# One bank left out before the value tiles, the branch to the exact maxima ahead of its tile's router steps, the last value tile copied by VectorE

## The chip, the core and the metric

The kernel runs on one core of one Trainium2 chip. The metric is the device time of one execution, in microseconds (us); of several executions the median counts. The engines are named as in the profile: PE (TensorE, the matrix unit; PEld are its weight loads), ACT (ScalarE), DVE (VectorE), POOL (GpSimd) and SP (SyncE, which here only issues DMAs). PSUM is the memory that PE writes; it has eight banks, and a tile of 128 partitions by 512 f32 fills one.

## The reference, cut to what is computed

The input x has 2048 tokens of width 1024. Three things come from it:

```
a = softmax(q k^T * 32^-0.5) v  @ wo      32 heads of width 32, q, k, v = x @ wqkv
b = sum over 32 heads of gelu(x . u[e]) * v[e],  e = the best of 64 experts
    (argmax of q1 k1^T over 8, argmax of q2 k2^T over 8)
g = sigmoid(sum(x * gate_w));   out = g * a + (1 - g) * b
```

## The kernel before, in words

All matmuls up to the attention are made in split precision: an operand is a high and a low part, and three products (high by high, high by low, low by high) are summed in one PSUM bank. x stays in SBUF as xh and xl. Tokens are cut into 16 tiles of 128 (NT = 16), the contraction into 8 chunks of 128 (KC = 8). A token tile therefore costs 8 x 3 = 24 matmuls of 128x128 by 512.

The stages follow each other in the order in which they are written; every engine works through its own instructions in that order, and semaphores tie the engines together.

1. q and k (lines 192 to 357): 16 chunks of 128 columns, each for four pieces of 512 tokens.
2. Router (lines 394 to 528): for each token tile t, `router_mm` (L394) makes the scores in a PSUM bank (matmuls at L401), and `router_step` (L450) makes four steps on DVE, ACT and POOL for the tiles t, t-1, t-2 and t-3. The step for tile t itself, `router_1` (L404 to L417), reads the bank: ACT copies a part (L405), DVE takes the maxima (L409 to L414). After tile 4 a bound on the attention scores is computed (`bound`). After tile 8 comes `exact_maxima` (L482): every engine loads that bound into a register (L484) and branches (L486). Only if the bound is above a limit does a loop over the heads run that takes exact maxima. With these inputs it isn't entered.
3. Values (lines 550 to 644): two halves of 512 columns. `values` (L550) makes the 24 matmuls of a tile (L558), `values_out` (L561) copies the bank to SBUF on ACT (L564; two buffers "vo") and issues the store on ACT's queue. In each half the first four tiles are made together, chunk by chunk (L619, L638). In the first half the last four (fin0, L626) are made together too. Between the halves ACT and DVE split the weights of the second half (`split_wv`, L631); only then, in ACT's order, are fin0's four banks copied (L636). The last tile of the second half is made in a bank of another pool (L643 and L644, tile "o"), because the pool ps1 with its eight banks is closed at L642.
4. Attention (lines 664 to 892): scores in a ring of seven banks (L714), exponentials on ACT (L724), the products with the values (L735).
5. Output projection (from L895).

PSUM banks are given out in turn by a counter (L97 to L102):

```
def bank():
    i = bank_no[0] % 8
    bank_no[0] += 1
    return ps1.tile([128, 512], F32, name=f"bk{i}")
```

A tile of a bank's name waits for the readers of that name's last tile. The stages up to the router take 80 banks, the router one for each tile and three beside (two in `bound`, one in `gate_sums`). The body of `exact_maxima` takes 65 (64 in its inner loops and one for a transpose) when the program is written, whether the branch is taken or not. At L637 the counter is rounded up to a multiple of eight. The tile "o" is the only one of a PSUM pool that is opened from the right end; the pools ps1 and the ring are laid from the left.

Of the kernel before, what the change touches and what calls it, by code (L numbers as in the profile page):

```python
# [9 lines left out]
F32 = mybir.dt.float32  # L10
F32R = mybir.dt.float32r
I32 = mybir.dt.int32
AF = mybir.ActivationFunctionType
# [7 lines left out]
NT = S // 128  # L21
# [9 lines left out]
def gated_mha_peer_kernel(ctx, tc, xT, wqkv, wv, wo, wq, k12, ug, v, out):  # L31
# [8 lines left out]
    nc = tc.nc  # L40
# [28 lines left out]
    def dma(dst, src, queue=nc.sync):  # L69
        a, b = (ap.bitcast(F32) if ap.dtype == F32R else ap for ap in (dst, src))  # L70
        return queue.dma_start(a, b)  # L71
# [16 lines left out]
    def split(hi, lo, src, on=None):  # L88
        nc.scalar.activation(hi, src, AF.Copy)  # L89
        (on or nc.vector).tensor_tensor(out=lo, in0=src, in1=hi.bitcast(F32), op=OP.subtract)  # L90
# [5 lines left out]
    ps1 = Pool("ps1", space=PSUM)  # L96
    bank_no = [0]  # L97
# [5 lines that stand above are left out]
# [215 lines left out]
    for k, (w, c) in enumerate(chunks):  # L318
        hi, lo = whl.pop((w, c))
        for n in range(NQ):  # L320
            ps = bank()
# [72 lines left out]
    def router_mm(t):  # L394
        ps = bank()
        for kc in range(KC):
            tok = slice(t * 128, (t + 1) * 128)
            wh, wl = Wp[kc]
            for a, b, first, last in ((xh, wh, kc == 0, False), (xh, wl, False, False),
                                      (xl, wh, False, kc == KC - 1)):  # L400
                nc.tensor.matmul(ps, a[:, kc, tok], b, start=first, stop=last)  # L401
        RT[t] = ps
# [47 lines left out]
    def router_step(t):  # L450
        for lag, f in ((3, router_4), (2, router_3), (1, router_2), (0, router_1)):
            if 0 <= t - lag < NT:
                f(t - lag)

    def bound():
        pb = bank()
        nc.tensor.matmul(pb[:H, 0:1], prf, ones[:, 0:1], start=True, stop=True)
        pb2 = bank()
        nc.tensor.matmul(pb2[:1, :H], ones[:, 0:1], prf, start=True, stop=True)
        nc.vector.tensor_reduce(cbits, pb2[:1, :H], axis=AX.X, op=OP.max)  # L460
        cneg = bw.tile([H, 1], F32, name="cneg")
        nc.scalar.activation(cneg, pb[:H, 0:1], AF.Copy, scale=-1.0)
        for r in range(2):
            sh = bw.tile([H, 512], F32R, name=f"sh{r}", bufs=1)
            if r == 0:
                nc.vector.tensor_copy(sh, cneg.to_broadcast([H, 512]))
            else:
                nc.vector.memset(sh.bitcast(F32), 0.0)
            dma(SHD[:, r, :].rearrange("h (n s) -> h n s", n=4), sh[:, None, :].to_broadcast([H, 4, 512]))

    def gate_sums():
        pz = bank()
        for qc in range(NQ):
            nc.tensor.matmul(pz[32 * qc:32 * qc + 32, :], ones, zacc[:, qc * 512:(qc + 1) * 512],
                             start=True, stop=True)
        zs = bw.tile([128, 512], F32, name="zs", bufs=1)
        nc.scalar.activation(zs, pz, AF.Copy)
        for qc in range(NQ):
            dma(ZD[:, qc * 512:(qc + 1) * 512], zs[32 * qc:32 * qc + 1, :])


    def exact_maxima():  # L482
        limit_bits = int(np.float32(SHIFT_LIMIT / SCALE).view(np.int32))
        creg = nc.values_load(cbits.bitcast(I32), min_val=0, max_val=2 ** 31 - 1,  # L484
                              skip_runtime_bounds_check_because="a float's bits without its sign")
        with tc.If(creg > limit_bits):  # L486
            with ExitStack() as st:
                gp = st.enter_context(tc.tile_pool(name="gp", bufs=1))
                with tc.For_i(0, H, 1) as h:
                    kt = gp.tile([96, S], F32R, name="gk")  # L490
                    hs, rows = bass.ds(h, 1), bass.ds(h * 32, 32)
                    for i, part in enumerate((0, 0, 1)):
                        dma(kt[32 * i:32 * i + 32, :], QKD[1][part][rows, :])
                    mx = gp.tile([128, NT, 4], F32, name="mx")
                    for t in range(NT):
                        if t % 8 == 0:
                            qt = gp.tile([96, S // 2], F32R, name="gq")
                            c = slice(t * 128, (t + 8) * 128)
                            for i, part in enumerate((0, 1, 0)):
                                dma(qt[32 * i:32 * i + 32, :], QKD[0][part][rows, c])  # L500
                        for n in range(4):
                            ps = bank()
                            nc.tensor.matmul(ps, qt[:, t % 8 * 128:(t % 8 + 1) * 128], kt[:, n * 512:(n + 1) * 512],
                                             start=True, stop=True)
                            nc.vector.tensor_reduce(mx[:, t, n:n + 1], ps, axis=AX.X, op=OP.max)
                    mr = gp.tile([128, NT], F32, name="mr")
                    nc.vector.tensor_reduce(mr, mx, axis=AX.X, op=OP.max, negate=True)
                    pt = bank()
                    nc.tensor.transpose(pt[:NT, :128], mr, ident)
                    hi = gp.tile([NT, 128], F32R, name="ghi")  # L510
                    lo = gp.tile([NT, 128], F32R, name="glo")
                    split(hi, lo, pt[:NT, :128])
                    for r, src in ((0, hi), (1, lo)):
                        dma(SHD[hs, r:r + 1, :].rearrange("a b (t s) -> (a b t) s", t=NT), src)

    for t in range(NT - 1):
        router_mm(t)
        router_step(t)
        if t == 4:
            bound()  # L520
        if t == 5:
            gate_sums()
            rz.close()
        if t == 8:
            exact_maxima()
    router_mm(NT - 1)
    rw.close()

# [21 lines left out]
    def values(ts, half, bank=bank):  # L550
        ps = [bank() for _ in ts]
        for kc in range(KC):
            wh, wl = WV[half, kc]
            for t, p in zip(ts, ps):
                tok = slice(t * 128, (t + 1) * 128)
                for a, b, first, last in ((xh, wh, kc == 0, False), (xh, wl, False, False),
                                          (xl, wh, False, kc == KC - 1)):
                    nc.tensor.matmul(p, a[:, kc, tok], b, start=first, stop=last)  # L558
        return ts, ps, half

    def values_out(ts, ps, half):  # L561
        for t, p in zip(ts, ps):
            o = vw.tile([128, 512], F32, name="vo")
            nc.scalar.activation(o, p, AF.Copy)  # L564
            dma(VD[half][t * 128:(t + 1) * 128, :], o, nc.scalar)

    def peer_act():
# [36 lines left out]
    def peer_turn(Ahl):  # L604
        for n in range(NQ):
            pt = bank()
            for t in range(4):
                nc.tensor.transpose(pt[:, t * 128:(t + 1) * 128],  # L608
                                    Ahl[:, 4 * n + t, :].bitcast(F32), ident)
            at = vw.tile([128, 512], F32R, name="at", bufs=1)  # L610
            nc.scalar.activation(at, pt, AF.Copy)
            dma(ATD[:, n * 512:(n + 1) * 512], at)
# [4 lines left out]
    zt = sm2.tile([NT, 128], F32, name="zt")  # L617
    dma(zt, ZD.rearrange("o (b m) -> (o b) m", m=128))
    values_out(*values(list(range(4)), 0))  # L619
    for t in range(4, NT - 4):  # L620
        values_out(*values([t], 0))
        if t == 5:
            Ahl = peer_act()
        if t == 10:
            peer_turn(Ahl)
# [8 lines left out]
    load_kq(0, Z)  # L634
    load_shift(0, Z)
    values_out(*fin0)  # L636
    bank_no[0] += -bank_no[0] % 8  # L637
    values_out(*values(list(range(4)), 1))  # L638
    for t in range(4, NT - 1):
        values_out(*values([t], 1))  # L640

    ps1.close()  # L642
    pso = Pool("pso", space=PSUM, side="right")  # L643
    values_out(*values([NT - 1], 1, lambda: pso.tile([128, 512], F32, name="o")))  # L644
    vw.close()
    sm2.close()
    sm.close()
# [403 lines left out]
```

## Time and profile before

| | |
|---|---|
| median of 3 runs | 1893.1 us (1891.32 to 1894.84) |
| profiled execution: its time, its span | 1894.6 us, 1892.8 us |
| PE busy | 1875.8 us (99%) |
| ACT busy | 1158.7 us (61%) |
| DVE busy | 1202.2 us (64%) |
| mean granted clock of TensorE | 0.998 |
| router's matmuls (L401), first and last start | 391.6 and 484.1 us |
| values' matmuls (L558), first and last start | 484.4 and 667.1 us |

Times in the trace count from the start of the span. A timeline row reads: start, duration, engine, line, operation, output <- input, shape, count, and in brackets how long the engine had been idle and who ended that. A row of a window gives for each engine the busy time in it and the number of instructions, and then PEclk, the clock granted to TensorE (1.00 is full). Matmuls overlap: one is shown with 0.39 us, but the next starts 0.23 us later.

### The profile page before, as it was taken

How to read it: one execution, taken by the hardware profiler on the slowest of the kernel's cores; microseconds unless marked ns; L12 is line 12 of the kernel's file. 1: busy time of each engine (PE TensorE's matmuls, PEld its weight loads, DVE VectorE, ACT ScalarE, POOL GpSimd, SP SyncE). 2: the span in 40 equal slices, each digit the busy share in tenths (PEclk: the TensorE clock that was granted, in tenths of full speed). 3: DMA queues.
4: the chain of work that ended last, by engine and by line, in shares of the span. 5: the costliest groups of instructions: out<-in, count | busy, mean ns of one | idle time of the engine just before them, and what ended most of it. 6: DMA issues, size and time to landing. Idle time of an engine off the chain costs nothing.

```text
span 1892.8 us, 25742 instructions
## 1 busy us (share of the span) xinstructions
PE 1875.8 (99%) x10271; PEld 1157.9 (61%) x10271; DVE 1202.2 (64%) x916; ACT 1158.7 (61%) x1413; POOL 148.6 (8%) x183
## 2 busy tenths in 40 slices
PE   9999999999998999999999999999999999999999
PEld 7877777887887844444444444444444444448887
DVE  4522224866520068888888888888888888895220
ACT  4211111200121189999999999999999999993110
POOL 0000000035200000000000000000000000010000
PEclk9999999999999999999999999999999999999999
DMA  5777774420222167777777776877777777756521
GB/s 211 278 270 254 264 271 137 137 73 2 79 88 79 46 161 166 160 172 159 175 169 183 167 184 157 184 162 184 170 176 170 164 166 179 188 128 172 154 89 67
DMA packets 108082, 302.72 MB, mean 160 GB/s; under 512 B 14724, under 2 KB 48660, under 8 KB 84472
## 3 DMA queue, kind: packets, MB, share of 16 engines
q1 hardware_dynamic: 70520, 154.76, 27.4%
q0 software_dynamic: 14976, 103.29, 26.3%
q10 hardware_dynamic: 22464, 43.00, 7.0%
q8 instruction: 81, 1.33, 0.3%
q14 instruction: 41, 0.34, 0.1%
HBM read 138.73 MB, written 62.66 MB: 106 GB/s over the span
## 4 chain that ended last, share of the span: by engine, by line
PE 76%; ACT 0%; DMA 0%; ACTq 0%; issue 0%; DVE 0%
PE ring L714 28%; PE o L735 25%; PE pa L918 9%; PE bk L558 9%; PE bk L401 2%; PE ring L748 1%; PE pa L927 1%; PE o L558 0%; ACT P L724 0%; PE o L748 0%; ACT vo L564 0%; DMA vd<-vo 0%; PE bk L608 0%; ACT accd L724 0%; ACTq L71 0%
## 5 line engine op out<-in xcount | busy, mean ns | idle before, releaser
L724 ACT ACTIVATE P<-ring 128x512 f32<-128x512 f32 (+2 forms) x1034 | 914.5, 984 | 14.9 <-PE o L735 1.4
L763 DVE TENSOR_TENSOR acc<-acc,P 128x2048 f32<-128x2048 f32 x319 | 730.9, 2291 | 74.1 <-ACT P L724 48.8
L735 PE MATMUL o<-P,V 128*32 128x512 f32 x3840 | 464.8, 599 | 0.0
L714 PE MATMUL ring<-z,z 98*128 98x512 f32 x1024 | 272.0, 407 | 1.3 <-ACT P L724 0.8
L714 PE MATMUL ring<-Q,K 98*128 98x512 f32 x1024 | 272.0, 407 | 0.9 <-ACT P L724 0.9
L714 PEld LDWEIGHTS ring<-Q,K 98*128 98x128 f32 x1024 | 182.0, 188 | 145.1 <-ACT P L724 75.1
L714 PEld LDWEIGHTS ring<-z,z 98*128 98x128 f32 x1024 | 182.1, 188 | 144.1 <-ACT P L724 75.1
L735 PEld LDWEIGHTS o<-P,V 128*32 128x32 f32 x3840 | 98.8, 109 | 223.2 <-issue 214.1
L89 ACT ACTIVATE hi<-bk 128x512 fp32r<-128x512 f32 x64 | 37.6, 598 | 242.6 <-PE bk L325 226.9
L325 PE MATMUL bk<-xh,whi 128*128 128x512 f32 x448 | 176.2, 393 | 0.1
L325 PE MATMUL bk<-xh,wlo 128*128 128x512 f32 x448 | 174.4, 389 | 0.0
L325 PE MATMUL bk<-xl,whi 128*128 128x512 f32 x448 | 174.4, 389 | 0.0
L757 POOL DMA_DIRECT2D accd<-P x95 | 81.5, 858 | 1104.8 <-ACT P L724 521.4
L90 DVE TENSOR_TENSOR lo<-bk,hi 128x512 fp32r<-128x512 f32 x64 | 44.1, 689 | 187.5 <-ACT hi L89 183.0
L761 DVE TENSOR_TENSOR acc<-P 128x2048 f32<-128x2048 f32 x32 | 73.4, 2293 | 77.2 <-ACT P L724 77.2
L558 PE MATMUL bk<-wvh,xh 128*128 128x512 f32 x248 | 97.6, 393 | 4.9 <-ACT vo L564 4.9
L325 PEld LDWEIGHTS bk<-xh,whi 128*128 128x128 f32 x448 | 84.1, 188 | 24.1 <-issue 6.7
L558 PE MATMUL bk<-wvl,xh 128*128 128x512 f32 x248 | 97.0, 391 | 0.0
L558 PE MATMUL bk<-wvh,xl 128*128 128x512 f32 x248 | 97.0, 391 | 0.0
L325 PEld LDWEIGHTS bk<-xh,wlo 128*128 128x128 f32 x448 | 84.1, 188 | 17.8
L325 PEld LDWEIGHTS bk<-xl,whi 128*128 128x128 f32 x448 | 84.1, 188 | 16.9
L564 ACT ACTIVATE vo<-bk 128x512 f32<-128x512 f32 x31 | 18.5, 597 | 115.6 <-PE bk L558 109.7
(163 smaller groups left out, 1662.4 us busy)
## 6 DMA issues: line engine op xcount, KB each, us to landing
accd<-P POOLq DMA_DIRECT2D x95, 1024.0 KB, 7.5
wqt<-in_wq SPq DMA_DIRECT2D x32, 1024.0 KB
vd<-vo ACTq DMA_DIRECT2D x32, 256.0 KB
z<-kdh SPq DMA_DIRECT2D x32, 256.0 KB
z<-qdh SPq DMA_DIRECT2D x32, 256.0 KB
V<-vd SPq DMA_DIRECT2D x32, 256.0 KB
K<-kdh SPq DMA_DIRECT2D x32, 256.0 KB
Q<-qdh SPq DMA_DIRECT2D x32, 256.0 KB
```

The lines of the kernel that those rows point to most:

```text
L89: nc.scalar.activation(hi, src, AF.Copy)
L90: (on or nc.vector).tensor_tensor(out=lo, in0=src, in1=hi.bitcast(F32), op=OP.subtract)
L325: nc.tensor.matmul(ps, a[:, kc, :], b[:, kc, n * 512:(n + 1) * 512], start=first, stop=last)
L401: nc.tensor.matmul(ps, a[:, kc, tok], b, start=first, stop=last)
L558: nc.tensor.matmul(p, a[:, kc, tok], b, start=first, stop=last)
L714: on_ring(nc.tensor.matmul(ring[:, i, :], K[:98, kt * 128:(kt + 1) * 128], Q[:98, qc * 512:(qc + 1) * 512], start=True, stop=True), i)
L724: on_ring(nc.scalar.activation(P[h, kt][:, q0 * 512:(q0 + m) * 512].rearrange("p (a m) -> p a m", a=m), ring[:, i:i + m, :], AF.Exp, scale ...
L735: nc.tensor.matmul(O[h][32 * qc:32 * qc + 32, :], Vt[g][:, kt, 32 * j:32 * j + 32], p[:, qc * 512:(qc + 1) * 512], start=(kt == 0), stop=( ...
L757: nc.gpsimd.dma_start(ACCD[h], P[h, kt], accum_op=OP.add)
L761: nc.vector.tensor_add(ACC[h], P[h, 0], P[h, kt])
L763: nc.vector.tensor_add(ACC[h], ACC[h], P[h, kt])
L918: nc.tensor.matmul(pa[tt, half], a[:, kc, tt * 128:(tt + 1) * 128], b[:, half * 512:(half + 1) * 512], start=(first and kc == kcs[0] and i ...
```

## The change

It has four parts. The body of `exact_maxima` takes its banks from a list of seven of its own, all but the bank that was given out last, and no longer moves the counter. The call of `exact_maxima` moves from behind `router_step(8)` to between `router_mm(8)` and `router_step(8)`. The counter moves one further after the first four value tiles of the first half, and is no longer rounded up between the halves. And the last value tile is copied by `nc.vector.tensor_copy` in place of ACT; its store is still issued on ACT's queue.

```
     limit_bits = ...
     creg = nc.values_load(cbits.bitcast(I32), ...)
+    banks = [(bank_no[0] + k) % 8 for k in range(7)]
+
+    def bank():
+        banks.append(banks.pop(0))
+        return ps1.tile([128, 512], F32, name=f"bk{banks[-1]}")
+
     with tc.If(creg > limit_bits):
...
 for t in range(NT - 1):
     router_mm(t)
+    if t == 8:
+        exact_maxima()
     router_step(t)
...
-    if t == 8:
-        exact_maxima()
...
-def values_out(ts, ps, half):
+def values_out(ts, ps, half, copy=lambda o, p: nc.scalar.activation(o, p, AF.Copy)):
     for t, p in zip(ts, ps):
         o = vw.tile([128, 512], F32, name="vo")
-        nc.scalar.activation(o, p, AF.Copy)
+        copy(o, p)
         dma(VD[half][t * 128:(t + 1) * 128, :], o, nc.scalar)
...
 values_out(*values(list(range(4)), 0))
+bank_no[0] += 1
 for t in range(4, NT - 4):
...
 values_out(*fin0)
-bank_no[0] += -bank_no[0] % 8
 values_out(*values(list(range(4)), 1))
...
-values_out(*values([NT - 1], 1, lambda: pso.tile([128, 512], F32, name="o")))
+values_out(*values([NT - 1], 1, lambda: pso.tile([128, 512], F32, name="o")),
+           nc.vector.tensor_copy)
```

## The prediction

> **What bounds the kernel now.** I read the page first (busy times, then the chain that ended last), then the view of waits for PE, then the timeline around each wait.
>
> ```profile
> span 1892.8 us, 25742 instructions
> PE 1875.8 (99%) x10271; PEld 1157.9 (61%) x10271; DVE 1202.2 (64%) x916; ACT 1158.7 (61%) x1413; POOL 148.6 (8%) x183
> ...
> PE 76%; ACT 0%; DMA 0%; ACTq 0%; issue 0%; DVE 0%
> ```
>
> PE is busy for 99% of the span and is nearly all of the chain. Time can come only from places where PE stands or is slowed. PE's waits name them:
>
> ```profile
> PE bk L558 <- ACT vo L564: 4.9, 1, 4.9
> PE bk L401 <- DVEq L486: 2.2, 1, 2.2
> PE ring L714 <- ACT P L724: 1.7, 3, 0.8
> ```
>
> The longest is one wait in the values (L558) for an ACT copy, the second one wait of the router (L401) for the branch at L486. The change touches both. First the branch:
>
> ```profile
> 438.66 0.22 DVE L414 TENSOR_SCALAR eq<-m 128x64 f32<-128x64 f32 x1
> ...
> 441.99 0.39 PE L401 MATMUL bk<-wph,xl 128*128 128x512 f32 x1
> ...
> 444.10 0.21 DVE L414 TENSOR_SCALAR eq<-m 128x64 f32<-128x64 f32 x1
> ...
> 444.59 0.47 PE L401 MATMUL bk<-wph,xh 128*128 128x512 f32 x1 [2.21 <-DVEq L486]
> 444.90 0.39 PE L401 MATMUL bk<-wpl,xh 128*128 128x512 f32 x1
> ...
> 449.22 0.39 PE L401 MATMUL bk<-wpl,xh 128*128 128x512 f32 x1
> ...
> 455.79 0.39 PE L401 MATMUL bk<-wph,xh 128*128 128x512 f32 x1
> ```
>
> ```profile
> L486 PEldq COMPARE_BRANCH  x1: 353/353/353, 438.7 to 438.7; - x1
> L486 PEldq EVENT_SEMAPHORE  x1: 51/51/51, 442.4 to 442.4; - x1
> ...
> L486 DVEq EVENT_SEMAPHORE  x1: 21/21/21, 444.4 to 444.4; - x1
> ```
>
> PE takes its branch at 438.7, while matmuls of tile 8 are still queued, and signals at 442.4, when the last of them (441.99 + 0.39) is done. DVE first finishes `router_1` of tile 8, whose last operation ends at 444.31, and signals at 444.4. PE's tile 9 waits for that signal, since its bank is one that DVE reads in the branch's body.
>
> The standstill is not all. In the windows the granted clock (the column PEclk, the third from the right) falls behind each long stop:
>
> ```profile
> 445.40:448.60 3.20, 3.20 (x9) 2.52 (x8) 1.80 (x3) 0.00 (x0) 2.19 (x4) 0.50 0.02 5
> ...
> 578.50:582.00 3.50, 3.39 (x8) 2.71 (x9) 0.00 (x0) 0.06 (x1) 0.00 (x0) 0.52 0.38 142
> 669.00:671.00 2.00, 1.03 (x4) 0.58 (x4) 0.73 (x1) 2.00 (x3) 0.00 (x0) 1.00 1.00 323
> 671.00:673.00 2.00, 1.62 (x8) 0.88 (x6) 0.00 (x0) 2.00 (x4) 0.00 (x0) 1.00 1.15 365
> ```
>
> So I price a stop from start to start, until the pace is even again. The even pace is (455.79 - 449.22) / 29 = 0.2266 us for each matmul. From 441.99 to 449.22 there are 13 starts, 13 x 0.2266 = 2.95 us at that pace; 7.23 us passed. The branch costs **4.28 us**, 2.4 of them standstill.
>
> Now the second place, between the halves of the values:
>
> ```profile
> 573.34 0.39 PE L558 MATMUL bk<-wvh,xl 128*128 128x512 f32 x1
> 578.61 0.79 PE L558 MATMUL bk<-wvh,xh 128*128 128x512 f32 x1 [4.88 <-ACT vo L564]
> ...
> 584.36 0.39 PE L558 MATMUL bk<-wvh,xh 128*128 128x512 f32 x1
> ```
>
> ```profile
> 573.76 0.63 ACT L89 ACTIVATE wvh<-wvraw 128x512 fp32r<-128x512 f32 x1 [2.09 <-PE bk L558]
> 574.30 0.58 ACT L564 ACTIVATE vo<-bk 128x512 f32<-128x512 f32 x1
> ...
> 577.96 0.60 ACT L564 ACTIVATE vo<-bk 128x512 f32<-128x512 f32 x1 [0.40 <-DMA vd<-vo]
> ```
>
> PE resumes 0.05 us after the fourth copy of fin0 (577.96 + 0.60 = 578.56). The counter explains it: 80 + 19 + 65 + 4 banks precede the fifth value tile, so fin0 gets banks 5, 6, 7, 0, and the rounding starts the second half at bank 0, the one copied last. From 573.34 to 584.36 there are 19 starts, 4.31 us at the even pace; 11.02 us passed. This stop costs **6.71 us**.
>
> **The change, part by part.**
>
> *Branch ahead of the router steps.* DVE now reaches the branch behind `router_1` of tile 7, whose last operation ends at 438.88, and signals within about 0.1 us, as it did behind 444.31. That is 3.4 us before PE is done with tile 8. ACT, too, has only its copy of tile 7 ahead of it. Nothing DVE does is delayed: it pays the crossing one tile earlier and then makes the same steps. Tile 8's bank is outside the body's list, so neither side waits for the other. What stays is PE's own signal, which can't come before tile 8's last matmul ends, at 442.38. From DVE's signal (444.4) to PE's next matmul (444.59) took 0.2 us, so PE would restart at about 442.6 in place of 442.22, and the first step after a stop is 0.31 us (444.59 to 444.90) instead of 0.23. I take 0.5 us for the rest. Gain 4.28 - 0.5 = **3.8 us**. The trace shows no branch without a waiting DVE: the ends are 0 (something else holds PE as long) and 4.3.
>
> *The counter.* Without the body's 65 the router's tiles 9 to 15 take banks 4, 5, 6, 7, 0, 1, 2, and the value tiles 3 to 6. With the one left out, the fifth value tile has bank 0, as before. Fin0 again gets 5, 6, 7, 0, but the second half starts at bank 1. Banks 1 to 4 were last read by the transposes of the peer part and by tile 11:
>
> ```profile
> 554.28 0.60 ACT L611 ACTIVATE at<-bk 128x512 fp32r<-128x512 f32 x1 [2.21 <-DMA atd<-at]
> ...
> 554.78 0.59 ACT L564 ACTIVATE vo<-bk 128x512 f32<-128x512 f32 x1
> ...
> 574.42 0.69 DVE L90 TENSOR_TENSOR wvl<-wvraw,wvh 128x512 fp32r<-128x512 f32 x1 [2.02 <-ACT wvh L89]
> ```
>
> All are read by 555.4, 18 us before they are wanted. Next in line are the weights. Their last split ends at 575.1 and is wanted seven chunks of 12 matmuls into the group, 573.57 + 84 x 0.2266 = 592.6. Fin0's banks, now copied beside matmuls, are wanted from 573.57 + 96 x 0.2266 = 595.3 on; the copies end at 578.6. Nothing takes the wait's place: gain **6.7 us**. The ends are 0 and 6.7.
>
> *What the counter brings at the end of the values.* Tile 14 now has bank 1 + 14 = 15, that is 7. The tile "o" for tile 15 is the one bank beside the ring's seven, the right end, which is bank 7 too. Before, that was tile 7's, and PE passed from tile 14 to "o" without a stop:
>
> ```profile
> 661.65 0.39 PE L558 MATMUL bk<-wvh,xl 128*128 128x512 f32 x1
> ...
> 661.88 0.39 PE L558 MATMUL o<-wvh,xh 128*128 128x512 f32 x1
> ...
> 662.08 0.60 ACT L564 ACTIVATE vo<-bk 128x512 f32<-128x512 f32 x1 [4.84 <-PE bk L558]
> ```
>
> Now PE must wait for that copy: 662.08 + 0.60 + 0.05 = 662.73 in place of 661.88, and a slow first step of 0.08: **0.9 us lost**. The ends are 0 (if "o" lies elsewhere) and 2.8, with a window at half clock as behind the branch.
>
> *The last copy on DVE.*
>
> ```profile
> 667.52 0.60 ACT L564 ACTIVATE vo<-o 128x512 f32<-128x512 f32 x1 [4.84 <-PE o L558]
> ...
> 668.15 0.33 ACTq L71 DMA_DIRECT2D vd<-vo  x1
> 668.57 1.94 ACT L724 ACTIVATE P<-ring 128x512 f32<-128x512 f32 x2 [0.46 <-PE ring L714]
> ...
> 670.57 0.96 PE L714 MATMUL ring<-z,z 98*128 98x512 f32 x3 [0.84 <-ACT P L724]
> ```
>
> ```profile
> L944 DVE COPY res<-pa 128x512 f32<-128x512 f32 x14 | 9.0, 682 | 18.4 <-PE pa L918 18.4
> ```
>
> The first exponential follows the copy and the issue of its store on ACT, and PE waits for it at 670.57. The copy leaves ACT, but the issue stays ahead of the exponentials and now waits for DVE, whose copy of that shape takes 682 ns to ACT's 597. Behind the waiting issue all of the attention's exponentials are queued. **0.1 us lost**; the ends are a gain of 0.6 (the whole copy gone from ACT's path) and a loss of 0.3. DVE has nothing else then but a memset for head 1.
>
> Sum: -3.8 - 6.7 + 0.9 + 0.1 = **-9.5 us**. Everything behind the values hangs on PE's last value matmul and moves with it. The profiled execution took 1894.6, which gives 1885.1; it lies 1.5 above the median of the runs shown, so I forecast 1893.1 - 9.5 = **1883.6 us**.
>
> *A rule of the Trainium skill.* The trace shows half clock for 3.2 us after only 2.2 us of standstill (the window 445.40 to 448.60). The Trainium skill, "TensorE: Matmul & The Clock Gate", in Part 1 on the clock gate, has the clock halved after at least one idle window of about 3.4 us. By that rule the branch's stop would have cost its 2.4 us alone, and the sum would be -7.6; the trace disagrees, since the slow matmuls are there.
>
> **The rivals.**
>
> 1. *Another wait lies under the branch's.* What PE did between 442.4 and 444.4 is covered by the wait for DVE; a refill of its queue or another engine's signal could be as late. For it: the branch is taken 3.3 us before PE can use what follows, and the trace can't show a shorter stop. Against it: PE moved 0.2 us after DVE's signal, and POOL wasn't waited for. The gain of 3.8 goes: -5.7, **1887.4 us**.
> 2. *A short stop halves the clock too.* The stops left are 0.4 and 0.85 us. Against it: the 0.84 us stop at 670.57 left the clock at 1.00 in the windows 669 to 671 and 671 to 673. If the later one did it, it would cost the branch's difference of 4.28 - 2.37 = 1.9 more: -7.6, **1885.5 us**. The same page, under "A second HAM failure mode: psum-queue depth-cycling", says that short idle times between groups of matmuls can make the clock oscillate; here that would be this case.
> 3. *"o" doesn't share tile 14's bank*: -10.4, **1882.7 us**.
> 4. *The counter doesn't do it:* the second half still waits for fin0's copies, by a wait on ACT's later count. The gain of 6.7 goes: -2.8, **1890.3 us**. Against it: the wait ended exactly with the copy of the bank in question.
> 5. *Slower: the ring doesn't make up the later first exponential.*
>
> ```profile
> 900.00:1100.00 200.00, 200.00 (x1247) 93.19 (x1247) 171.15 (x80) 194.74 (x227) 16.29 (x19) 1.00 0.77 176
> ...
> PEld ring L714 <- ACT P L724: 146.6, 193, 1.1
> ```
>
> In the attention ACT is busy for 194.74 of 200 us, and 193 times a weight load of the ring waits for an exponential, 0.76 us on average, under matmuls that still run. If the 0.12 us by which the exponentials start later stayed, and showed at each of these, it would be 193 x 0.12 = 23 us: 1893.1 - 9.5 + 23 = **1906.6 us**; from 79 such waits on, the gain is eaten. Against it: ACT has 5.3 us free in 200, which makes up 0.12 us within some 5 us, and PE itself waited for it three times in all.
>
> **How the numbers follow.** Forecast 0.70; rivals 1 to 5: 0.12, 0.07, 0.05, 0.03, 0.03. A difference of 0.2% (3.8 us) is about what a measurement of this kernel can tell from no change. The forecast and rivals 1 to 3 are faster by more: 0.94. Rival 4 is within it: 0.03. Rival 5 is slower: 0.03. The runs before spread by about 1.8 us to either side. The range goes from rival 3 less that spread, 1881, to rival 1 with a part of it, 1888.5; it takes in the ends of the last two parts and leaves out rivals 4 and 5 and some spread.
>
> **What would show it.** In the profile after: no wait of PE for L486 above about 0.5 us, and PEclk 1.00 around it; no wait at the second half's start, fin0's copies beside running matmuls; one new wait of PE for the copy of L564 of about 0.85 us, just before the matmuls into "o", at full clock; a DVE copy of about 0.68 us into vo, and the first exponential about 1.2 us after PE's last value matmul ends. Wrong would be a PE wait of over 1 us at the branch, any wait of the second half's first group, or more PE waits in the ring.

## The result

The changed kernel takes 1884.48 us (median of 5 runs, 1884.09 to 1886.32), the kernel before beside it 1894.16 us (1891.32 to 1894.84): a ratio of 0.9953, with a 95% interval of 0.9939 to 0.9968. A second measurement on another occasion (run e8 below) gave 0.9969 (0.9956 to 0.9982). The forecast was 1883.6 us, 0.9950. The profiled execution took 1886.32 us with a span of 1884.6.

First the view of PE's waits after (line, who released it: us in total, times, longest):

```profile
PE bk L211 <- ACT xh L89: 1.6, 1, 1.6
PE bk L207 <- DVE ident L85: 1.4, 1, 1.4
PE ring L725 <- ACT P L735: 1.3, 3, 0.8
PE o L566 <- ACT vo L569: 0.7, 1, 0.7
PE ring L725 <- ACT accd L735: 0.4, 1, 0.4
PE bk L401 <- ACT xu L405: 0.3, 1, 0.3
```

The two waits on which the forecast rested (4.9 us for fin0's copies, 2.2 us for DVE at the branch) are gone. Two small ones are new: 0.7 us before the tile "o" and 0.3 us behind tile 8. The lines have moved: the branch is L493 now, the value matmuls are L566, their copies L569 (ACT) and L572 (DVE), the ring is L725.

The branch, in the view of its line and in the timeline of PE:

```profile
L493 DVEq EVENT_SEMAPHORE  x1: 21/21/21, 439.1 to 439.1; - x1
...
L493 PEldq EVENT_SEMAPHORE  x1: 51/51/51, 442.5 to 442.5; - x1
```

```profile
442.06 0.39 PE L401 MATMUL bk<-wph,xl 128*128 128x512 f32 x1
442.74 0.47 PE L401 MATMUL bk<-wph,xh 128*128 128x512 f32 x1 [0.30 <-ACT xu L405]
443.05 0.40 PE L401 MATMUL bk<-wpl,xh 128*128 128x512 f32 x1
```

DVE signals at 439.1, PE at 442.5, when tile 8's last matmul is done, and the next matmul starts 0.24 us later. From 442.06 to tile 15's last start at 480.72 lie 168 starts, and 38.66 us passed. Where the branch is left out (e7 below), the same 168 starts take 38.08 us. The stop costs 0.58 us.

The end of the values in PE's timeline, and then the handover to the attention:

```profile
651.54 0.39 PE L566 MATMUL bk<-wvh,xl 128*128 128x512 f32 x1
652.61 0.50 PE L566 MATMUL o<-wvh,xh 128*128 128x512 f32 x1 [0.69 <-ACT vo L569]
...
657.96 0.39 PE L566 MATMUL o<-wvh,xl 128*128 128x512 f32 x1
```

```profile
658.44 0.69 DVE L572 COPY vo<-o 128x512 f32<-128x512 f32 x1 [86.72 <-PE o L566]
659.17 0.33 ACTq L71 DMA_DIRECT2D vd<-vo  x1
659.54 1.94 ACT L735 ACTIVATE P<-ring 128x512 f32<-128x512 f32 x2 [6.98 <-PE ring L725]
```

Tile 14 and "o" do share a bank: from 651.54 to 657.96 there are 24 starts, 5.44 us at the even pace, and 6.42 passed, a loss of 0.98. The first exponential starts 1.58 us after PE's last value matmul starts; before it was 668.57 - 667.09 = 1.48.

One thing the forecast didn't have stands in the windows (the third column from the right is PEclk):

```profile
659.61:663.02 3.41, 1.97 (x7) 0.82 (x6) 1.76 (x1) 3.41 (x4) 0.00 (x0) 1.00 0.95 296
663.02:666.43 3.41, 3.41 (x13) 1.64 (x17) 1.25 (x1) 3.41 (x5) 0.00 (x0) 0.50 1.13 288
```

At the ring's start the clock was halved for 3.41 us in this execution; it wasn't in the profile before. In the chain of work the ring's groups show the price:

```profile
659.54 1.94 ACT P L735 x2
...
667.71 2.04 PE ring L725 x8
```

From the first exponential to that group of eight 8.17 us passed. The same group in the chain of before:

```profile
675.24 2.04 PE ring L714 x8
```

There it was 675.24 - 668.57 = 6.67. So the profiled execution is 9.0 us ahead at the first exponential (668.57 to 659.54), 7.5 at the ring's third group, and 8.2 at its end. The last 0.7 us is nearly all one stop that the profile before has in the middle of the ring and the profile after hasn't: PE waits 0.68 us for an exponential and resumes at 1173.94. The second profile of the changed kernel (e8) has such a stop too, of 0.50 us and at another place.

### The profile page after: what moved, and what is told of

Same layout as the page of the kernel before. It is cut to its first block, busy times and chain, and to the rows that moved or that the text cites. A ratio compares the mean times of both kernels' runs of the same rounds, so it can differ in the third digit from the quotient of the medians.

```text
span 1884.6 us, 25741 instructions
## 1 busy us (share of the span) xinstructions
PE 1874.6 (99%) x10271; PEld 1157.2 (61%) x10271; DVE 1203.3 (64%) x917; ACT 1158.3 (61%) x1412; POOL 148.6 (8%) x183
## 4 chain that ended last, share of the span: by engine, by line
PE 99%; ACT 0%; DMA 0%; DVE 0%; issue 0%; ACTq 0%; DVEq 0%
PE ring L725 28%; PE o L746 25%; PE bk L325 16%; PE pa L929 9%; PE bk L566 9%; PE bk L401 5%; PE bk L211 2%; PE bk L272 2%; PE ring L759 1%; PE pa L938 1%; PE o L566 0%; DMA w0raw<-in_wqkv 0%; PE bk L286 0%; PE o L759 0%; ACT P L735 0%
## 5 line engine op out<-in xcount | busy, mean ns | idle before, releaser
L725 PE MATMUL ring<-z,z 98*128 98x512 f32 x1024 | 273.0, 408 | 1.4 <-ACT P L735 1.1
L725 PE MATMUL ring<-Q,K 98*128 98x512 f32 x1024 | 272.0, 407 | 0.2 <-ACT P L735 0.2
L725 PEld LDWEIGHTS ring<-z,z 98*128 98x128 f32 x1024 | 182.6, 188 | 144.4 <-ACT P L735 75.4
L725 PEld LDWEIGHTS ring<-Q,K 98*128 98x128 f32 x1024 | 182.0, 188 | 144.3 <-ACT P L735 72.7
L566 PE MATMUL bk<-wvh,xh 128*128 128x512 f32 x248 | 96.7, 390 | 0.0
L566 PE MATMUL bk<-wvh,xl 128*128 128x512 f32 x248 | 96.5, 389 | 0.0
L566 PE MATMUL bk<-wvl,xh 128*128 128x512 f32 x248 | 96.5, 389 | 0.0
L569 ACT ACTIVATE vo<-bk 128x512 f32<-128x512 f32 x31 | 18.5, 597 | 109.3 <-PE bk L566 103.4
```

What stands on the lines that cost most here:

```text
L725: on_ring(nc.tensor.matmul(ring[:, i, :], K[:98, kt * 128:(kt + 1) * 128], Q[:98, qc * 512:(qc + 1) * 512], start=True, stop=True), i)
```

## The experiments

The ratio is to runs of the kernel before beside each kernel; "last value start" is the start of PE's last value matmul in the profile (before 667.09, after 657.96).

| run | median us (range) | ratio, 95% interval | last value start |
|---|---|---|---|
| e1 branch alone | 1890.74 (1889.54 to 1896.06) | 0.9991 (0.9982 to 1.0001) | 663.96 |
| e2 counter alone | 1887.67 (1886.42 to 1889.05) | 0.9967 (0.9955 to 0.998) | 661.24 |
| e3 changed, no bank left out | 1885.25 (1883.66 to 1886.28) | 0.9956 (0.9942 to 0.9969) | 656.88 |
| e4 as e3, ACT copies | 1885.1 (1883.25 to 1886.06) | 0.9952 (0.9938 to 0.9965) | 657.04 |
| e5 before, PE busy between the halves | 1893.33 (1891.9 to 1895.18) | 0.9998 (0.9989 to 1.0008) | 666.40 |
| e6 as e3, store on POOL's queue | 1882.58 (1882.29 to 1882.88) | 0.9943 (0.993 to 0.9957) | 656.82 |
| e7 as e4, no branch | 1885.83 (1884.21 to 1887.02) | 0.9961 (0.9948 to 0.9974) | 656.43 |
| e8 the changed kernel again | 1887.28 (1885.51 to 1888.78) | 0.9969 (0.9956 to 0.9982) | 657.59 |
| e9 only the halves' stop, PE busy in it | 1888.07 (1887.38 to 1889.11) | 0.9966 (0.9952 to 0.9979) | 662.08 |
| e10 only the halves' stop | 1890.03 (1889.12 to 1890.92) | 0.9976 (0.9967 to 0.9985) | 664.82 |

e1 to e4, e5 to e8, and e9 and e10 were measured on three occasions, with the kernel before at 1894.1, 1893.08 and 1894.78 us; between occasions compare the ratios. The edits of e1, e3, e4 and e6 start from the changed kernel, that of e7 from e4, and those of e2 and e5 from the kernel before.

My theory was that of the prediction, with the sizes read from the trace after: three independent terms at PE, a small one at ACT, and the clock. The first rival was that the terms are not independent.

**e1, the branch alone.**

```
     if t == 8:
         exact_maxima()
+        bank_no[0] += 65
...
-    bank_no[0] += 1            # before the fifth value tile
...
+    bank_no[0] += -bank_no[0] % 8
...
-               nc.vector.tensor_copy)
```

> The kernel before with the branch ahead of router_step(8) alone; the counter moves on by 65 behind it, so all later banks and the rounding are those of before. Theory (three independent terms): PE's stop at the branch shrinks from 4.1 us (standstill and half clock) to 0.6, so about 3.5 us faster than before (ratio 0.9982); the 4.9 us wait between the value halves stays, with its half clock behind it (6.7 us in all). Rival (what the branch frees is lost again at the next wait, the value halves): no change in time, and a wait between the halves that is longer by 3.5 us.

By the time alone this is open: the interval ends at 1.0001, and the runs spread over 6.5 us. The profile decides. The stop at the branch costs 0.58 us, and the wait between the halves is as long as ever, not 3.5 us longer:

```profile
PE bk L566 <- ACT vo L569: 4.9, 1, 4.9
```

PE's last value matmul starts 3.1 us earlier, not 3.5, because the half clock behind that wait lasted twice as long here (the second of these windows; in the profile before it was 3.41 us):

```profile
568.92:572.33 3.41, 1.31 (x6) 0.75 (x4) 0.69 (x1) 1.67 (x3) 0.00 (x0) 1.00 0.11 26
572.33:579.16 6.83, 4.04 (x10) 3.17 (x11) 0.00 (x0) 1.24 (x3) 0.00 (x0) 0.50 0.40 149
```

e1 keeps the branch body's own list of banks; whether the branch could move as cheaply without that list was not tested.

The spread, too, goes with the clock. The four runs above 1894 us have a mean granted clock of 0.996, the seven others (1889.5 to 1892.1) one of 0.998 or 0.999.

**e2, the counter alone.**

```
 values_out(*fin0)
-bank_no[0] += -bank_no[0] % 8
 values_out(*values(list(range(4)), 1))
```

> The kernel before without the rounding of the counter alone, so that the second half starts at bank 1; the branch and the copy stay. Theory: the 6.7 us between the halves go, the stop before the tile o (about 1.0 us) comes, the branch's 4.1 us stay: 5.7 us faster (ratio 0.9970). Rival (the gain came from the two changes together): under 2 us faster.

```profile
PE bk L401 <- DVEq L486: 2.2, 1, 2.2
PE ring L713 <- ACT P L723: 1.5, 3, 0.8
...
PE o L558 <- ACT vo L564: 0.7, 1, 0.7
```

The wait between the halves is gone, the one before "o" has come, the branch's has stayed. The last value start is 5.85 us earlier, the medians differ by 6.4. Without the rounding, and with nothing else changed, the longest wait is gone: the rounding was its cause. In the sum, 3.1 from e1 and 5.85 from e2 make 9.0, and both parts together gave 9.13.

**e3 and e4, without the bank left out, and then with ACT's copy too.**

```
 values_out(*values(list(range(4)), 0))
-bank_no[0] += 1
 for t in range(4, NT - 4):
```

```
 values_out(*values([NT - 1], 1, lambda: pso.tile([128, 512], F32, name="o")),
-           nc.vector.tensor_copy)
```

> The changed kernel without the bank that is left out. Then fin0 has banks 4 to 7, the second half starts at bank 0, tile 14 has bank 6 and o shares a bank with tile 7. Theory: PE's stop before o (0.7 us in the waits, 1.0 us from start to start) is gone and nothing else: 10.2 us faster than before in place of 9.5 (ratio 0.9947). Rival (PE waits for ACT's copy of tile 14 by some other tie): the stop stays, ratio 0.9950.

> As the run before it, and the last value tile copied by ACT again, so that only the branch and the counter are changed. Theory: from PE's last value matmul to the first exponential 1.48 us as in before, not 1.58: 0.1 us faster than with DVE's copy, too little for the clock on the wall. Rival (the DVE copy lets the exponentials start earlier): 1.48 us or more here against less with DVE.

In both, PE's wait before "o" isn't there, and the last value start comes 1.1 and 0.9 us earlier than in the changed kernel. The left-out bank thus only costs: it puts tile 14 into the bank of "o". The first exponential starts 1.58 us behind the last value start with DVE's copy (e3) and 1.48 us with ACT's (e4). The times can't tell either difference, as expected for the second; for the first I had expected a ratio of 0.9947 in e3 and got 0.9956, within the interval. That e3 and e4 aren't plainly faster may again be the clock, which is not shown: e4's profile has the half clock at the ring's start, e3's hasn't (below).

**e5, PE kept busy between the halves.**

```
     bank_no[0] += -bank_no[0] % 8
+    busy = ps1.tile([128, 512], F32, name="bk1")
+    for i in range(20):
+        nc.tensor.matmul(busy, xh[:, 0, :128], xh[:, 0, :512], start=True, stop=True)
     values_out(*values(list(range(4)), 1))
```

> The kernel before, and in the wait between the halves PE makes 20 matmuls that nobody reads (20 x 0.227 = 4.5 of the 4.9 us of the wait, in bank 1). Theory (the matmuls behind the wait are slow because the clock fell while PE stood): the second half starts at the same place, 5.3 us after the first half's last matmul, but at full pace at once, PEclk 1.00: 6.7 us of cost become about 5.1, 1.6 us faster in the trace (ratio 0.9991, within what the times can tell). Rival (they are slow because the queue refills behind a wait): the slow matmuls stay, no gain.

In PE's timeline the matmuls behind the wait now come at full pace at once:

```profile
574.17 0.39 PE L558 MATMUL bk<-wvh,xl 128*128 128x512 f32 x1
574.39 4.70 PE L640 MATMUL bk<-xh 128*128 128x512 f32 x20
579.45 0.50 PE L558 MATMUL bk<-wvh,xh 128*128 128x512 f32 x1 [0.36 <-ACT vo L564]
579.78 0.39 PE L558 MATMUL bk<-wvl,xh 128*128 128x512 f32 x1
```

The wait is as long (5.28 us from start to start), the slow matmuls are gone, and the stop costs 5.2 us instead of 6.7. The rival is out. But the time shows no gain (0.9998, with an interval that still takes in the 0.9991 expected). In the profiled execution the half clock came at the ring's start instead, which took 1.5 us back; whether that was chance, e5 left open. e9 and e10 try it without the longer stops at the ring's start.

**e6, the last store off ACT's queue.**

```
-def values_out(ts, ps, half, copy=...):
+def values_out(ts, ps, half, queue=nc.scalar, copy=...):
...
-        dma(VD[half][t * 128:(t + 1) * 128, :], o, nc.scalar)
+        dma(VD[half][t * 128:(t + 1) * 128, :], o, queue)
...
-           nc.vector.tensor_copy)
+           nc.gpsimd, nc.vector.tensor_copy)
```

> The changed kernel without the bank that is left out (e3), and the last tile's store issued on POOL's queue in place of ACT's, so that ACT has nothing of the last tile to do. Theory: the first exponential waits for its first score bank alone and starts about 0.6 us after PE's last value matmul starts in place of 1.58; PE's stops at the ring's start (0.23, 0.84 and 0.38 us) shrink by about 0.9 in sum, and the half clock that some executions show there comes less often: 0.9 to 2.5 us faster than e3. Rival (the exponentials wait for the memory of the copied tile, or for the keys of head 0): start at 1.5 us as before, no gain.

```profile
657.30 0.69 DVE L572 COPY vo<-o 128x512 f32<-128x512 f32 x1 [85.74 <-PE o L566]
657.48 2.15 ACT L734 ACTIVATE P<-ring 128x512 f32<-128x512 f32 x2 [5.07 <-PE ring L724]
658.29 0.58 POOL L71 DMA_DIRECT2D vd<-vo  x1 [165.08 <-PE ring L724]
```

The first exponential now starts 0.66 us after the last value start (656.82), before the copy is done. PE's stops at the ring's start shrink from 1.45 us in sum to 1.01 (0.63 and 0.38), less than I expected; the ring's third group comes 7.54 us after the last value start, in e3 8.25. All five runs lie within 0.6 us, and this is the fastest kernel of the study: 1882.58 us, against 1887.28 of the changed kernel beside it. Part of that difference is the stop before "o", which e3 removes as well, and part the half clock, which e6's profile doesn't have at the ring's start. DVE's copy gains nothing while the store is issued on ACT's queue (e3 against e4). ACT's copy with the store on POOL's queue wasn't tried, so the shares of the two in e6's gain are not shown.

**e7, no branch.**

```
     router_mm(t)
-    if t == 8:
-        exact_maxima()
     router_step(t)
```

> The kernel e4 without the branch: exact_maxima is left out, and with it the exact maxima that would be taken if the bound were above its limit. Theory: the 0.57 us that PE still loses there is its own signal and the branch; without it the tiles follow each other at 0.227 us and 0.6 us are gained on e4. Rival (the rest is a wait for ACT, which the profile names as releaser): the gap of 0.68 us stays.

```profile
442.10 0.39 PE L401 MATMUL bk<-wph,xl 128*128 128x512 f32 x1
442.33 0.39 PE L401 MATMUL bk<-wph,xh 128*128 128x512 f32 x1
442.55 0.39 PE L401 MATMUL bk<-wpl,xh 128*128 128x512 f32 x1
```

The tiles follow each other without a gap, and the last value start is 0.61 us earlier than in e4. The rest at the branch is the branch's own; ACT, which the profile names as releaser, only ended at the same time. The median is 0.7 us above e4's, so the time doesn't show it.

**e8, the changed kernel again.**

> The changed kernel once more, for a second profile of the same program. Theory (the half clock at the ring's start depends on where PE's short stops fall in the clock's own period): the stops of 0.23, 0.84 and 0.38 us are there again, and the half clock behind them may be there or not; where an execution has a mean clock of 1.000 it is 1.5 to 2 us shorter than one of 0.998. Rival (the half clock comes from the change itself): it is there in each profile of this kernel.

The half clock at the ring's start is there again, at 663.22 to 666.63, so this run alone doesn't refute its rival. But of the ten runs of the changed kernel in both measurements the four at a mean clock of 1.000 are the one of 1885.51 here and three of 1884.09 to 1884.65, and the four at 0.998 took 1886.32 to 1888.78. One half clock of 3.41 us takes 3.41 x 0.5 / 1885 = 0.0009 off the mean, so the runs at 1.000 had none of that length, while the profiled one at 0.998 had two, at 7.66 and at 663.02: the same program with and without. Where the other runs had theirs is not on record. The medians of the two measurements, 2.8 us apart, differ in the same way (one of five at 0.998 there, three of five here).

**e9 and e10, only the stop between the halves left.** Both have e1's branch and rounding and e6's copy and store; e9 has e5's 20 matmuls besides.

> The kernel with the branch moved (e1) and the last store on POOL's queue (as e6), so that only the wait between the halves is left as a long stop, and in it the 20 matmuls that nobody reads. Theory: the wait stays, the half clock behind it doesn't, and no other stop is long enough to bring it elsewhere: 5.2 us above e6 (about 1888), with a spread as narrow as e6's (under 1 us), and 1.5 to 1.9 us below the run beside it. Rival (what the filling saves is given back elsewhere): the same time as the run beside it.

> The same without the 20 matmuls. Theory: 6.7 to 7.1 us above e6 (about 1889.5), the half clock behind the wait for 3.4 or 6.8 us, by where the wait falls in the clock's period of 3.41 us. Rival: as the run beside it.

e9 takes 1888.07 us, e10 1890.03, and every run of e9 is below every run of e10 (1889.11 at most, 1889.12 at least). So 2.0 us of what the wait between the halves costs is the slow matmuls behind it: in e9's profile the clock stays at 1.00 there, in e10's it is at 0.50 for 6.83 us. In e5's profiled execution the gain was given back at the ring's start, where e9's stops are shorter (1.01 us in sum). e9 lies 5.5 us above e6, which was measured on another occasion; 5.2 was expected.

## Why the prediction was right

| step | forecast | measured in the trace | told apart by |
|---|---|---|---|
| branch | -3.8 | 4.06 to 0.58: -3.5 | e1, e7 |
| counter | -6.7 | -6.7 | e2 |
| stop before "o" | +0.9 | +0.98 | e3 |
| last copy | +0.1 | +0.10 | e4 |
| half clock at the ring's start | none | +1.5 in the profiled execution | e3, e4, e6, e8 |

**The bounds.** PE's waits were the right view: each wait removed moved PE's later work by its price, and no other wait took its place (in e1 the longer half clock took 0.4 us back). At the first exponential the profiled execution is 9.0 us ahead, where the same steps had made 9.5. That the medians came still closer, 9.7 us apart on the first occasion, is partly luck: on the second (e8) they are 5.8 us apart, with more runs at the lower clock.

**The branch.** The mechanism held: DVE's signal was the bound, and now comes 3.4 us ahead of PE's. The size was off by 0.3 us. I had counted 13 starts from 441.99 to 449.22, and there are 14, so the stop had cost 4.06 us and not 4.28 (the whole stretch of 168 starts, from 441.99 to 484.13, gives 42.14 - 38.08 = 4.06, with the 38.08 us of e7). The rest is 0.58 instead of 0.5. Rival 1, another wait under the branch's, is refuted by e1 and e7.

**The counter, "o" and the copy** came out within 0.1 us, and rivals 3 and 4 are refuted: PE waits before "o" until tile 14 is copied (e3 takes the wait away), and the counter alone removes the wait between the halves (e2). For the copy the reason given held as well: the store's issue on ACT's queue stays ahead of the exponentials. e6 removes just that, and the exponentials start 0.9 us earlier.

**The half clock.** Rival 2 said that a short stop could halve the clock. I had set against it one stop of 0.84 us that didn't, and given it 0.07. For the places named (the branch's rest, "o") it is false: neither is followed by half clock in any of the nine profiles that have one of them (after, e1 to e4, e6 and e8 to e10). For the ring's start it is true in four profiles of twelve (after, e4, e5 and e8). What tells these four from the other eight is not the length of one stop but the sum of PE's idle time in one period of the clock; the last section has it, and a period elsewhere that doesn't fit. The step that failed is the sentence that everything behind the values moves with PE's last value matmul: the ring's start doesn't, by up to 1.5 us, from execution to execution.

**Rival 5**, a ring that doesn't make up a later start, is refuted: PE waits three times for P in the ring's whole length, as before (four times in e8, 1.8 us in all).

## What to carry to other kernels

Where PE is the bound, price a stop from start to start until the pace is even again, and not by the wait alone: here the clock behind it added 1.7 us to each of two waits. A round-robin of banks is part of the schedule: which bank comes after a stage's last evacuated one, and which tile had the bank that the next pool opens, decides over whole waits, and can be counted by hand. Moving a copy to a free engine frees the busy one only if the DMA issue that waits for the copy leaves its queue too.

## What the runs showed of the hardware that I had not expected

The granted clock falls and rises in steps of one period. Every stretch of half clock found in these stages lasted 3.41 us, or 6.83 behind the wait between the halves in e1 and e10. Within one execution their starts lie whole periods apart: in before 445.31 and 578.43, which is 39.0 times 3.413; in the changed kernel 7.66 and 663.02, 192.0 times; in e5 446.33 and 671.61, 66.0 times. So the periods can be laid over a trace, and PE's idle time counted in each. These are periods that ended without and with a fall, in the windows of before, e3, e4 and e5 (the first number behind the comma is PE's busy time in 3.41 us; the row after it is the period that followed):

```profile
667.17:670.59 3.42, 2.45 (x11) 1.45 (x9) 1.76 (x1) 2.61 (x4) 0.00 (x0) 1.00 0.49 154
670.59:674.00 3.41, 3.03 (x16) 1.61 (x20) 0.00 (x0) 3.41 (x4) 0.00 (x0) 1.00 1.15 343
```

```profile
659.76:663.17 3.41, 2.33 (x8) 1.34 (x8) 0.55 (x1) 3.41 (x5) 0.00 (x0) 1.00 1.11 348
663.17:666.59 3.42, 3.42 (x24) 1.67 (x24) 2.29 (x1) 3.42 (x5) 0.38 (x1) 1.00 1.06 234
```

```profile
659.39:662.80 3.41, 2.19 (x8) 1.16 (x7) 0.29 (x1) 3.41 (x5) 0.00 (x0) 1.00 1.10 347
662.80:666.22 3.42, 3.42 (x19) 0.88 (x17) 2.06 (x1) 3.16 (x3) 0.00 (x0) 0.50 1.06 254
```

```profile
668.20:671.61 3.41, 2.06 (x7) 1.02 (x7) 0.84 (x1) 3.41 (x5) 0.00 (x0) 1.00 1.01 301
671.61:675.02 3.41, 3.41 (x13) 1.28 (x15) 1.50 (x1) 3.41 (x5) 0.00 (x0) 0.50 1.11 287
```

With 0.97 us (28%) and 1.08 us (32%) idle the clock stayed; with 1.22 us (36%), 1.35 us (40%) and, in the changed kernel, 1.44 us (42%) it fell. At the ring's start this parts all twelve profiles: at most 1.08 us idle in the eight without the half clock, at least 1.22 us in the four with it. The same stops there (0.84 and 0.38 us, and 0.23 with DVE's copy) fall into one period or are divided between two, by where the period lies in that execution, and that makes the difference.

But the share of idle time is not the whole rule. These are two periods of e5 at the kernel's start and two of before at the wait between the halves:

```profile
12.84:16.25 3.41, 1.99 (x7) 1.03 (x7) 2.76 (x5) 2.27 (x3) 0.00 (x0) 1.00 0.93 345
16.25:19.66 3.41, 3.41 (x15) 2.83 (x16) 2.25 (x4) 2.83 (x4) 0.00 (x0) 1.00 1.03 426
```

```profile
571.60:575.02 3.42, 2.13 (x10) 1.43 (x8) 1.29 (x2) 1.19 (x3) 0.00 (x0) 1.00 0.32 72
575.02:578.43 3.41, 0.00 (x0) 0.00 (x0) 0.10 (x1) 1.66 (x3) 0.00 (x0) 1.00 0.42 156
```

The first of each pair is idle for 1.42 us (42%) and 1.29 us (38%), more than e4's period that was followed by a fall, and yet the clock stays at 1.00 through the next. In before it falls only behind the wholly idle period, at 578.43. What else decides is open. The matmuls of these two stages are 128*128 and those of the ring 98*128; whether that counts was not tested, and no experiment varied the idle time alone.

The Trainium skill, "TensorE: Matmul & The Clock Gate", Part 1, gives a free-running window of 3413 ns, and the trace agrees to 0.01 us. The same page of the Trainium skill has the clock fall after an idle window, and at the ring's start the trace disagrees, since there a window that is idle for little more than a third was enough.
